# One score chunk in the row-sum banks and one split out-projection step between values and scores

## The chip, the cores and the metric

The kernel runs on one core of one Trainium2 chip. The metric is the device time of one execution in microseconds (us). The core's engines work side by side, each through its own queue in program order: TensorE (PE, matrix products; its weight loads are shown apart as PEld), ScalarE (ACT, here exponentials and Gelu), VectorE (DVE, copies, products, reciprocals), GpSimd (POOL, here masks and the issuing of loads) and SyncE (SP, here the stores and the transposing loads). They wait for each other on semaphores.

## The reference

Attention over eight batches with eight heads, 576 tokens and 64 numbers a head, with 16 "beacon" keys put before the 576 own keys, and a causal mask on the own keys; then a gated feed-forward block over all 4608 tokens. Cut to what matters:

```python
k_all = np.concatenate([beacon_k, k], axis=2)          # 592 keys
v_all = np.concatenate([beacon_v, v], axis=2)
scores = scale * np.matmul(q, k_all.transpose(0, 1, 3, 2))
scores = np.where(causal, -1000000000.0, scores)
a = np.exp(scores - scores.max(-1, keepdims=True))
a /= a.sum(-1, keepdims=True) + 1e-09
attn = np.matmul(a, v_all)                             # (8, 8, 576, 64)
x = attn.transpose(0, 2, 1, 3).reshape(4608, 512)
g, val = x @ w_gate, x @ w_val                         # 512 -> 1536
out = (0.5 * g * (1.0 + erf(g / sqrt(2))) * val) @ w_out   # 1536 -> 512
```

## The kernel before, in words

**Stages.** The kernel takes the batches b = 0 to 7 one after the other. Each has an attention, which leaves 576 columns of `xT_sb` (the transposed input of the feed-forward block), and behind it the twelve gate and value products (`gate_val`) of one chunk of 512 tokens. Nine chunks make 4608 tokens, so that the ninth comes at the very end. The out-projection is cut into units: `o(n)` (line 412) issues the next n units, each one matmul of 128 hidden numbers by 512 outputs; twelve units fill one PSUM bank (tag `o`), and with the twelfth a DVE copy (line 432) and a store are issued. The units of one chunk are strewn into the attention of the next batch, where they fill PE while ACT works. `o(n, cols=64)` (line 421) does a unit as two matmuls, each over half of the array's columns and half of the output's partitions, which run side by side.

**An attention.** Heads are taken in pairs, m = 0 to 3. A pair's scores are made transposed, keys in the partitions, in four chunks (`CHUNKS`, line 31). The order of work is written out by hand as strings that `attention` (line 457) reads step by step, one string a pair and a fifth for the end:

- `Sc`: the scores of chunk c of the pair (`scores`, line 258): matmuls of 64 rows of the array, one for each head of the pair, into a pair of PSUM banks of the pool `s`, which has two such buffers; then one exponential on ACT from there into `expT`; and in batches 2 to 7 the masks of the chunk's diagonal tiles on POOL (`mask`, line 281; the last pair's last chunk is masked on DVE instead). Chunk 0 has the diagonal of key tile 0, chunk 1 those of tiles 2 and 4, chunk 2 that of tile 1, chunk 3 that of tile 3.
- `sc`: the same, with the score banks taken from the tag `z` of another pool, which has one buffer.
- `Zm`: the sums over the keys (`sums`, line 322), with ones as weights, and the values of the first 64 queries. Its two banks are the tag `z`. It takes the key tiles in the order 0, 2, 4, 1, 3 (`attend`, line 305) with matmuls that use 64 columns of the array.
- `Im`: the reciprocals of the sums on DVE (`invert`): a transpose, a reciprocal, a transpose.
- `Vm`: values times weights into the tag `x` (64 columns of the array, too). `Mm`: two DVE products that bring sums and values together (`scale`, line 349); they free `z` and `x`.
- `On`: n units of the out-projection. `Pn`: n units with half the columns each.
- `Nn`: POOL issues n loads of the batch after (`load_next`). In batch 7 nothing is left to load.

Every engine's queue has exactly the order in which these steps are issued. In each of the pairs 1 to 3, then, PE does scores 0 and 1 of pair m, sums and values of pair m-1, scores 2 and 3 of pair m, and then out-projection units. Scores 2 and 3 use the buffers that scores 0 and 1 had, and so wait for the exponentials of those.

For the score banks the rule is in these lines:

```python
s_ps = (psum_s if tag == "s" else psum_x).tile([P, 2, 512], FP32, name="s_ps", tag=tag)
act(expT[:, :, o : o + w], s_ps[:, :, 0:w], ACT.Exp, scale=QK_SCALE)
```

Of the kernel before, what the change touches and what calls it, by code (L numbers as in the profile page):

```python
# [45 lines left out]
Z0 = 448  # L46
# [12 lines left out]
def kernel(  # L59
# [64 lines left out]
    def load_runs(b, m):  # L124
        for out_ap, in_ap in runs(b, m):
            dma(out_ap, in_ap)
# [59 lines left out]
    def load_v_tile(b, t):  # L186
        if t == 0:
            load_beacon(dma, flat(v_ring[b % 2])[0:NB, 0, :], beacon_v[b])
        r0, n = (NB, 112) if t == 0 else (0, KROWS[t])
        dma(v_ring[b % 2][r0 : r0 + n, t, :, :], v[b, :, S_LO[t] : S_LO[t] + n, :].rearrange("h p d -> p h d"))  # L190
# [24 lines left out]
    def heat(n, tag="o"):  # L215
        if n == 0:
            return
        t = bank(tag, FP32, CH, "heat")
        for _ in range(2 * n):
            mm(t[:, 0 : CH // 2], warm[:, 0:P], warm, True, True)  # L220
# [31 lines left out]
    def trans_in(tag, b, m, w):  # L252
        t_ps = bank(tag, BF16, 1024, "t_ps")
        trans(b, m, w, t_ps, [(S, dve_copy)])
# [3 lines left out]
    def scores(b, m, *chunks, tag="s"):  # L258
        i = b * NPAIR + m
        qkT = qk_ring[b % 2]  # L260
        for c in chunks:
            if c == 0:
                exp_of[i] = epool.tile([P, 2, EXP_W], BF16, name="expT", tag="expT")
            expT = exp_of[i]
            s_ps = (psum_s if tag == "s" else psum_x).tile([P, 2, 512], FP32, name="s_ps", tag=tag)
            for t, s_lo, w, col in CHUNKS[c]:
                for hi in range(2):
                    r = slice(64 * hi, 64 * hi + 64)
                    mm(
                        s_ps[:, hi, col : col + w],  # L270
                        qkT[r, 1, m, t * P : (t + 1) * P],
                        qkT[r, 0, m, NB + s_lo : NB + s_lo + w],
                        True,
                        True,
                    )
            o, w = CHUNK_OFF[c], CHUNK_W[c]
            act(expT[:, :, o : o + w], s_ps[:, :, 0:w], ACT.Exp, scale=QK_SCALE)
            if b > 1:
                mask(b, m, c, by_table=m == NPAIR - 1 and c == len(CHUNKS) - 1)
# [42 lines left out]
    def sums(b, m):  # L322
        z_ps = z_of[b * NPAIR + m] = psum_x.tile([P, 1024], FP32, name="z_ps", tag="z")
        attend(b, m, z_ps, Z0, True, 0, SPLIT)
        attend(b, m, z_ps, Z0 + SPLIT, True, SPLIT, S)
        attend(b, m, z_ps, 0, False, 0, SPLIT, start=False)

    def values(b, m):
        x_ps = x_of[b * NPAIR + m] = psum_x.tile([P, S - SPLIT], FP32, name="x_ps", tag="x")
        attend(b, m, x_ps, 0, False, SPLIT, S)  # L330
# [3 lines left out]
    def invert(b, m):  # L334

        i = b * NPAIR + m
        zt = npool.tile([P, S], FP32, name="zt", tag="zt")
        keep(nc.vector.transpose(zt, z_of[i][:, Z0 : Z0 + S]))  # L338
        rz = npool.tile([P, NBLK], FP32, name="rz", tag="rz")
        keep(nc.vector.reciprocal(rz, zt.rearrange("p (n j) -> p n j", j=32)[:, :, 0]))  # L340
        rec = npool.tile([P, S], FP32, name="rec", tag="rec")
        keep(
            nc.vector.transpose(  # L343
                rec.rearrange("p (n j) -> p n j", j=32), rz.unsqueeze(2).to_broadcast([P, NBLK, 32])
            )
        )
        rec_of[i] = rec

    def scale(b, m):
        i = b * NPAIR + m  # L350
        rec = rec_of.pop(i)
        del exp_of[i]
        for acc, q0, q1 in ((z_of.pop(i), 0, SPLIT), (x_of.pop(i), SPLIT, S)):
            keep(
                nc.vector.tensor_tensor(  # L355
                    out=xT_sb[:, m, b * S + q0 : b * S + q1],
                    in0=acc[:, 0 : q1 - q0],
                    in1=rec[:, q0:q1],
                    op=ALU.mult,
                )  # L360
            )
# [50 lines left out]
    def o(n, tags="o", cols=P):  # L412


        for _ in range(n):
            ci, u = divmod(out_done[0], OUT_UNITS)
            ti, fi = divmod(u, F_TILES)
            if fi == 0:
                o_ps_of[0] = bank(tags[out_done[0] // F_TILES % len(tags)], FP32, D_MODEL, "o_ps")
            o_ps = o_ps_of[0][:, 0:D_MODEL]  # L420
            for c0 in range(0, P, cols):
                mm(
                    o_ps[c0 : c0 + cols],
                    h_of[ci][:, fi, ti * P + c0 : ti * P + c0 + cols],
                    wo_sb[:, fi, :],
                    fi == 0,
                    fi == F_TILES - 1,
                    skip_group_check=True,
                )
            if fi == F_TILES - 1:  # L430
                o_sb = opool.tile([P, D_MODEL], FP32, name="o_sb", tag="o_sb")
                keep(nc.vector.tensor_copy(o_sb, o_ps))  # L432
                n0 = ci * CH + ti * P
                keep(nc.sync.dma_start(out=out[n0 : n0 + P, :], in_=o_sb))
            out_done[0] += 1
# [15 lines left out]
    def exp_table():  # L451
        keep(nc.scalar.preload_act_table_set(SET_EXP))

    def gelu_table():
        keep(nc.scalar.preload_act_table_set(SET_GELU))

    def attention(b, *slots, extra=None):


        for m, slot in enumerate(slots):  # L460
            for step in slot.split():
                kind, n = step[0], step[1:]
                if kind == "S":
                    scores(b, m, *(int(c) for c in n))
                elif kind == "s":
                    scores(b, m, *(int(c) for c in n), tag="z")
                elif kind == "Z":
                    sums(b, int(n or m - 1))
                    if not n:
                        invert(b, m - 1)  # L470
                elif kind == "I":
                    invert(b, int(n))
                elif kind == "V":
                    values(b, int(n or m - 1))
                    if not n:
                        scale(b, m - 1)
                elif kind == "M":
                    scale(b, int(n))
                elif kind == "O":
                    o(int(n))  # L480
                elif kind == "P":
                    o(int(n), cols=P // 2)
                elif kind in "adkq":
                    extra[kind](b, *n)
                else:
                    extra[kind](*n) if kind in "kqrwLhyad" else extra[kind](n)
# [40 lines left out]
    def load_next(n):  # L527
        for _ in range(min(n, len(queue))):
            dma(*queue.pop(0))

    W_CUT = ((0, 512), (512, 1024), (1024, 1536))
    extra = {
        "k": lambda b, m, tag: trans_in(tag, b, int(m), 1),
        "q": lambda b, m, tag: trans_in(tag, b, int(m), 0),
        "a": lambda b, m, c: mask(b, int(m), int(c)),
        "d": lambda b, m, c: mask(b, int(m), int(c), by_table=True),
        "r": lambda m: load_runs(0, int(m)),
        "h": lambda n, tag: heat(int(n), tag),
        "y": lambda t: load_v_tile(0, int(t)),
        "N": lambda n: load_next(int(n)),  # L540
# [3 lines left out]
    for m in range(1, NPAIR):  # L544
# [4 lines left out]
        extra=extra,  # L549
# [12 lines left out]
    for b in range(1, B):  # L562
        exp_table()
        if b + 1 < B:
            queue.extend(qk_loads(b + 1))
        if b == 1:
            attention(b, "k1x S0 N3 S1 a01 k3z d00 q1x S2 a02 s3 q2o d03", "S0 S1 k2o Z0 a11 S2 I0 a12 V0 a10 M0 S3", "a13 S0 q3o S1 a21 Z1 S2 a20 I1 S3 a22 V1", "M1 S0 S1 a23 Z2 I2 V2 a31 M2 a30 S2 a32 S3 d33 O12", "Z3 I3 V3 M3 O12 N3 N3", extra=extra)
        elif b == 2:
            attention(b, "O12 s0 S1 S2 O12 S3 N3", "S0 S1 Z0 I0 V0 M0 S2 S3 O12 N3", "S0 S1 Z1 I1 V1 M1 S2 S3 O12 N3", "S0 S1 Z2 I2 V2 M2 S2 S3 O12 N2", "Z3 I3 V3 M3", extra=extra)
        else:  # L570
            attention(b, "O7 s0 S1 S2 O12 S3 N3", "S0 S1 Z0 I0 V0 M0 S2 S3 O12 N3", "S0 S1 Z1 I1 V1 M1 S2 S3 O7 N3", "S0 S1 Z2 I2 V2 M2 S2 S3 P5 N2", "Z3 I3 V3 M3", extra=extra)
        gelu_table()
        if b + 1 < B:
            load_next(99)
            load_v(b + 1)
        gate_val_first(b, o, 0 if b == 1 else 5 if b == 2 else 5)
        if b + 1 < B:
            xbar_transpose(b + 1)
        gate_val(b, 1, F_TILES)
# [36 lines left out]
```

## Time and profile before

| | |
|---|---|
| time, median of 4 runs | 396.21 us (396.01 to 396.74) |
| profiled execution, its own time | 396.2 us |
| its span, first to last instruction | 394.5 us |
| mean granted TensorE clock | 0.995 |
| PE busy | 379.2 us (96%) |
| DVE, ACT, POOL busy | 198.0, 188.1, 161.1 us |
| attention of batch 4, first score to first gate product | 179.28 to 198.32 us |
| attention of batch 7 | 306.65 to 325.68 us |

Rows of the profile give the line of the kernel, the engine, the operation, output and inputs by name, the tile's shape and the count, then busy time and the mean duration. `64*128` before a matmul's shape is rows by columns of the array that it uses. Almost all matmuls are issued by the helper of line 203, so that they are told apart by their outputs: `s_ps` scores, `z_ps` sums, `x_ps` values, `o_ps` out-projection, `gv_ps` gate and value. A row of the timeline gives the start, the length from the first start to the last end, the engine, and in brackets how long the engine had been idle and for what; neighbouring instructions of one kind are merged and bear the shape of the first. A matmul's row ends when its result is there, while the next one starts long before that: what a matmul costs in a row of matmuls is the distance of the starts (0.216 us for an out-projection unit, whose own row has 0.379).

### The profile page before, as it was taken

What the parts mean: (1) busy time and instruction counts of PE and PEld (TensorE: products, weight loads), DVE (VectorE), ACT (ScalarE), POOL (GpSimd) and SP (SyncE); (2) the same over time, 40 slices, a digit from 0 to 9 for tenths busy, and PEclk for the clock granted to TensorE, in tenths of its full rate; (3) what the DMA queues carried; (4) which work ended last, traced back from release to release, by engine and by line L of the source; (5) the groups of instructions that cost most, each with busy time, mean ns of one, the idle gap of its engine ahead of it and who ended that gap; (6) DMA issues with size and microseconds to landing.
All of it is one profiled execution on the core that took longest, in us unless ns stands there. A gap on an engine that the chain in (4) does not pass through costs nothing.

```text
span 394.5 us, 6776 instructions
## 1 busy us (share of the span) xinstructions
PE 379.2 (96%) x2672; PEld 180.2 (46%) x2713; DVE 198.0 (50%) x346; ACT 188.1 (48%) x255; POOL 161.1 (41%) x292
## 2 busy tenths in 40 slices
PE   7899989999999999999999999999999999999996
PEld 4544454444444444444444444444444444444443
DVE  4674587343664448344654367345733475333332
ACT  4653394337633566338733764356533772322210
POOL 8877248503970079204950299008920330000000
PEclk9899999999999999999999999999999999999999
DMA  9999957971999059922995099907991100000012
GB/s 138 165 206 189 179 33 69 166 99 57 107 148 130 0 83 142 155 36 65 112 158 82 28 121 131 135 17 84 138 143 34 56 28 27 0 28 27 28 61 100
DMA packets 139424, 36.50 MB, mean 93 GB/s; under 512 B 126976, under 2 KB 134912, under 8 KB 139392
## 3 DMA queue, kind: packets, MB, share of 16 engines
q0 software_dynamic: 103696, 18.85, 62.8%
q1 hardware_dynamic: 35552, 17.08, 20.2%
q8 instruction: 21, 0.34, 0.4%
q10 hardware_dynamic: 144, 0.13, 0.1%
q14 instruction: 11, 0.09, 0.1%
HBM read 38.27 MB, written 9.44 MB: 121 GB/s over the span
## 4 chain that ended last, share of the span: by engine, by line
PE 89%; DVE 4%; ACT 2%; issue 1%; DMA 1%; POOL 1%; POOLq 0%
PE gv_ps L203 47%; PE o_ps L203 24%; PE z_ps L203 7%; PE s_ps L203 5%; PE x_ps L203 5%; ACT expT L206 2%; DMA k<-in_k_dram 1%; DVE o_sb L432 1%; DVE rec L343 1%; DVE zt L338 1%; PE t_ps L224 1%; DVE xT_sb L355 0%; DVE qkT L247 0%; POOL q L115 0%; DVE rz L340 0%
## 5 line engine op out<-in xcount | busy, mean ns | idle before, releaser
L206 ACT ACTIVATE ge_sb<-gv_ps 128x512 bf16<-128x512 f32 x108 | 64.4, 597 | 152.3 <-PE gv_ps L203 152.3
L390 DVE TENSOR_TENSOR hT_sb<-gv_ps,ge_sb 128x512 bf16<-128x512 f32 x108 | 74.6, 691 | 120.2 <-ACT ge_sb L206 120.2
L206 ACT ACTIVATE expT<-s_ps 128x1024 bf16<-128x1024 f32 (+3 forms) x128 | 102.4, 864 | 31.9 <-PE s_ps L203 30.1
L294 POOL TENSOR_SCALAR_AFFINE_SELECT expT<-expT 128x256 bf16<-128x256 bf16 (+2 forms) x149 | 54.2, 395 | 149.5 <-ACT expT L206 147.5
L203 PE MATMUL gv_ps<-xT_sb,wv_sb 128*128 128x512 bf16 x423 | 111.7, 379 | 0.5
L203 PE MATMUL gv_ps<-xT_sb,wg_sb 128*128 128x512 bf16 x423 | 111.6, 379 | 0.6 <-issue 0.2
L203 PE MATMUL o_ps<-wo_sb,hT_sb 128*128 128x512 bf16 (+2 forms) x446 | 99.7, 374 | 1.5
L203 PEld LDWEIGHTS <-wv_sb 128*128 128x128 bf16 x432 | 42.3, 98 | 50.9
L203 PEld LDWEIGHTS <-wg_sb 128*128 128x128 bf16 x432 | 41.6, 98 | 50.8 <-issue 1.9
L203 PEld LDWEIGHTS <-hT_sb 128*128 128x128 bf16 (+1 forms) x469 | 42.1, 99 | 48.6 <-issue 3.5
L203 PE MATMUL s_ps<-qkT 64*128 64x80 bf16 (+5 forms) x384 | 37.7, 284 | 5.5 <-ACT expT L206 4.5
L432 DVE COPY o_sb<-o_ps 128x512 f32<-128x512 f32 x35 | 24.1, 689 | 36.2 <-PE o_ps L203 34.8
L338 DVE STREAM_TRANSPOSE zt<-z_ps 128x576 f32<-128x576 f32 x32 | 25.0, 781 | 23.7 <-PE z_ps L203 23.7
L115 POOL DMA_DIRECT2D v_sb<-in_v_dram x40 | 33.9, 883 | 0.0
L203 PE MATMUL z_ps<-expT,ones 80*64 80x80 bf16 (+5 forms) x384 | 30.1, 290 | 0.5 <-DVE xT_sb L355 0.3
L115 POOL DMA_DIRECT2D k_sb<-in_k_dram x30 | 25.7, 856 | 7.7 <-DMA wo_sb<-in_moe_w_out_dram 7.4
L203 PEld LDWEIGHTS <-qkT 64*128 64x128 bf16 x384 | 13.9, 94 | 32.2 <-issue 28.4
L203 PE MATMUL x_ps<-expT,v_sb 128*64 128x512 bf16 (+4 forms) x320 | 27.5, 300 | 0.0
L115 POOL DMA_DIRECT2D q_sb<-in_q_dram x30 | 25.9, 863 | 0.3
L343 DVE STREAM_TRANSPOSE rec<-rz 128x576 f32<-128x576 f32 x32 | 24.9, 778 | 1.1
L355 DVE TENSOR_TENSOR xT_sb<-x_ps,rec 128x512 bf16<-128x512 f32 x32 | 21.8, 680 | 0.8 <-PE x_ps L203 0.8
L203 PEld LDWEIGHTS <-ones 128*64 128x64 bf16 (+1 forms) x384 | 15.4, 111 | 12.5 <-issue 6.5
(39 smaller groups left out, 125.5 us busy)
## 6 DMA issues: line engine op xcount, KB each, us to landing
out_dram<-o_sb SPq DMA_DIRECT2D x35, 256.0 KB, 2.0
v_sb<-in_v_dram POOLq DMA_DIRECT2D x24, 128.0 KB, 6.9
q_sb<-in_q_dram POOLq DMA_DIRECT2D x24, 128.0 KB, 4.3
k_sb<-in_k_dram POOLq DMA_DIRECT2D x18, 128.0 KB, 4.4
wg_sb<-in_moe_w_gate_dram POOLq DMA_DIRECT2D x3, 512.0 KB, 7.5
wv_sb<-in_moe_w_val_dram POOLq DMA_DIRECT2D x3, 512.0 KB, 9.7
wo_sb<-in_moe_w_out_dram POOLq DMA_DIRECT2D x1, 1536.0 KB, 13.4
q<-in_q_dram POOLq DMA_DIRECT2D x7, 144.0 KB, 5.3
```

The source lines that it names most:

```text
L115: keep(nc.gpsimd.dma_start(out=out_ap, in_=in_ap))
L203: keep(nc.tensor.matmul(out_ap, lhsT, rhs, start=start, stop=stop, **kw))
L206: keep(nc.scalar.activation(out_ap, in_ap, func, **kw))
L224: keep(nc.tensor.transpose(out_ap, in_ap, ident[0:n, 0:n]))
L294: nc.gpsimd.affine_select(out=d, in_=d, pattern=[[0, 2], [1, DIAG[t]]], compare_op=ALU.is_ge, fill=0.0, base=base, channel_multiplier=-1,)
L338: keep(nc.vector.transpose(zt, z_of[i][:, Z0 : Z0 + S]))
L343: nc.vector.transpose(rec.rearrange("p (n j) -> p n j", j=32), rz.unsqueeze(2).to_broadcast([P, NBLK, 32]))
L355: nc.vector.tensor_tensor(out=xT_sb[:, m, b * S + q0 : b * S + q1], in0=acc[:, 0 : q1 - q0], in1=rec[:, q0:q1], op=ALU.mult,)
L390: nc.vector.tensor_tensor(out=h_of[ci][:, fi, :], in0=gv_ps[:, 1, :], in1=ge_sb, op=ALU.mult)
L432: keep(nc.vector.tensor_copy(o_sb, o_ps))
```

## The change

In the attentions of batches 2 to 7, chunk 3 of pair 0 gets its score banks from the tag `z` (`s3` in place of `S3`). In pairs 1 to 3 one out-projection unit in the half-column form (`P1`) is put between the values of the pair before and scores 2, and the number of units behind scores 3 is changed: one fewer in pairs 1 and 2 of batch 2 and in pair 1 of the others; two fewer in pair 2 of batches 3 to 7; in pair 3, 11 units and these in half-column form for batch 2, and the same five for batches 3 to 7. Each attention issues as many units as before: 60 in batch 2, 43 in the others. The instructions on DVE, ACT, POOL and SP and their order stay as they are.

```diff
         elif b == 2:
-            attention(b, "O12 s0 S1 S2 O12 S3 N3", "S0 S1 Z0 I0 V0 M0 S2 S3 O12 N3", "S0 S1 Z1 I1 V1 M1 S2 S3 O12 N3", "S0 S1 Z2 I2 V2 M2 S2 S3 O12 N2", "Z3 I3 V3 M3", extra=extra)
+            attention(b, "O12 s0 S1 S2 O12 s3 N3", "S0 S1 Z0 I0 V0 M0 P1 S2 S3 O11 N3", "S0 S1 Z1 I1 V1 M1 P1 S2 S3 O11 N3", "S0 S1 Z2 I2 V2 M2 P1 S2 S3 P11 N2", "Z3 I3 V3 M3", extra=extra)
         else:
-            attention(b, "O7 s0 S1 S2 O12 S3 N3", "S0 S1 Z0 I0 V0 M0 S2 S3 O12 N3", "S0 S1 Z1 I1 V1 M1 S2 S3 O7 N3", "S0 S1 Z2 I2 V2 M2 S2 S3 P5 N2", "Z3 I3 V3 M3", extra=extra)
+            attention(b, "O7 s0 S1 S2 O12 s3 N3", "S0 S1 Z0 I0 V0 M0 P1 S2 S3 O11 N3", "S0 S1 Z1 I1 V1 M1 P1 S2 S3 O5 N3", "S0 S1 Z2 I2 V2 M2 P1 S2 S3 P5 N2", "Z3 I3 V3 M3", extra=extra)
```

## The prediction

> **What bounds the kernel now.** The page first: PE is busy for 96% of the span at a clock of 0.995, and the chain that ended last, by engine, is PE:
>
> ```profile
> PE 89%; DVE 4%; ACT 2%; issue 1%; DMA 1%; POOL 1%; POOLq 0%
> ```
>
> No matmul is taken away, so only PE's waits inside the changed attentions can give time. The list of waits has them all:
>
> ```profile
> PE s_ps L203 <- ACT expT L206: 4.5, 13, 0.4
> ```
>
> It counts only idle time after the modelled end of a matmul, so I read the starts instead, in batch 4's timeline (batches 2, 3, 5, 6, 7 repeat it within 0.01 us where I say nothing else). Around pair 0's end, PE, ACT and POOL:
>
> ```profile
> 182.81 0.48 PE L203 MATMUL s_ps<-qkT 64*128 64x208 bf16 x4
> 183.69 0.38 PE L203 MATMUL s_ps<-qkT 64*128 64x64 bf16 x6 [0.39 <-ACT expT L206]
> 184.00 0.22 PE L203 MATMUL z_ps<-expT,ones 128*64 128x64 bf16 x2
> ...
> 183.12 0.52 ACT L206 ACTIVATE expT<-s_ps 128x416 bf16<-128x416 f32 x1 [0.61 <-PE s_ps L203]
> ...
> 183.70 0.41 POOL L294 TENSOR_SCALAR_AFFINE_SELECT expT<-expT 128x256 bf16<-128x256 bf16 x1 [0.73 <-ACT expT L206]
> ```
>
> The first row is S3 of pair 0 and S0 of pair 1 (S0 starts at 182.91). S1 of pair 1 wants the buffer of S3 and starts 0.05 after S3's exponential ends (183.64). In pairs 2 and 3, where it does not wait so, S1 follows S0 by 0.22. So it would start at 183.14: it waits 0.55 us. The sums Z0 follow at 184.00. Tile 3's mask, on POOL, is done at 184.11.
>
> The second wait is in pairs 2 and 3. S2 starts at 190.72, and S3 (208 wide) at 191.07:
>
> ```profile
> 190.72 0.61 PE L203 MATMUL s_ps<-qkT 64*128 64x464 bf16 x4
> 191.07 0.27 PE L203 MATMUL s_ps<-qkT 64*128 64x208 bf16 x2
> 191.27 1.69 PE L203 MATMUL o_ps<-wo_sb,hT_sb 128*128 128x512 bf16 x6
> ...
> 191.13 0.94 ACT L206 ACTIVATE expT<-s_ps 128x928 bf16<-128x928 f32 x1
> ```
>
> S3 starts 0.34 behind S2; in pair 1 it is 0.20. The missing 0.14 is S1's exponential, which ends at 191.02, 0.05 before.
>
> The third place is the end, where Z3 needs the masks of pair 3. POOL's queue, from pair 2's masks on:
>
> ```profile
> 191.09 1.87 POOL L294 TENSOR_SCALAR_AFFINE_SELECT expT<-expT 128x224 bf16<-128x224 bf16 x5
> 193.04 0.90 POOL L115 DMA_DIRECT2D q_sb<-in_q_dram  x1
> 193.92 0.89 POOL L115 DMA_DIRECT2D k_sb<-in_k_dram  x1
> 194.78 0.90 POOL L115 DMA_DIRECT2D q_sb<-in_q_dram  x1
> ...
> 196.64 0.43 POOL L294 TENSOR_SCALAR_AFFINE_SELECT expT<-expT 128x256 bf16<-128x256 bf16 x1
> ```
>
> and PE and DVE beside it:
>
> ```profile
> 196.69 0.98 PE L203 MATMUL z_ps<-expT,ones 128*64 128x64 bf16 x12
> ...
> 197.12 0.55 PE L203 MATMUL z_ps<-expT,ones 128*64 128x464 bf16 x4
> ...
> 196.32 0.22 DVE L355 TENSOR_TENSOR xT_sb<-z_ps,rec 128x64 bf16<-128x64 f32 x1
> ```
>
> POOL has no pause from 191.09 to 197.07. Z3's matmul over tile 1 starts at 197.12, 0.05 behind the end of tile 1's mask. The same distance is there in every batch that loads: 154.61 and 154.67 in batch 3, 239.53 and 239.58 in 5, 281.98 and 282.04 in 6. Only batch 7, without loads, has room (mask end 324.16, matmul 324.48), and batch 2, with longer pairs (mask end 110.45, Z3 at 111.85). So in batches 3 to 6 PE and POOL arrive together, and this decides what PE's earlier gains are worth.
>
> **The change, part by part, in batch 4.**
>
> *s3.* S1 of pair 1 now takes the buffer of S2, whose exponential ended at 182.51, and starts at 183.14. The wait does not vanish: Z0 wants the `z` banks, held by S3 until 183.64. S1's three pairs of matmuls take 0.30 (188.87 to 189.17 in pair 2), so Z0 would be ready at 183.44. What it loses after the release: S1's wait cost 0.05. But Z0 waits with its weight load for the banks, as Z3 does, and that row is nearer: DVE's product ends at 196.54, Z3 starts at 196.69, 0.15 later. I take 0.15: Z0 at 183.78, a gain of 0.22 (0.31 with 0.05). Behind Z0 nothing new waits: its last matmul, 0.65 on, needs tile 3's mask, which ends at 184.11.
>
> *P1.* Behind the values the array is already cut into 64 columns. Values to scores costs 0.096 beyond the 0.087 of the last value matmul (0.183 between starts), and that change of shape is there once before and once after. P1 adds the distance of two such units, 0.213 to 0.216 (row of P5, 195.75 to 195.96), against 0.216 for the unit it replaces; so nothing on its own. Its two weight loads per unit are 0.110 each, the whole-array one 0.098; in P5's row they lie beside the matmuls. P1 opens a new bank in pair 1: the copy that frees it ends at 183.61, P1 comes at 185.24. In pair 2 (batch 2) and the others the bank was freed as early or is already open. No DMA is issued by a unit but the store at a bank's twelfth, which stays at the end of a pair, so SP's queue is passed by nothing, and POOL's loads keep their place behind the masks.
> The Trainium skill, "TensorEngine Tiling (Array Packing)", section Tile-to-Partition Mapping (Restrictions), says that column tiling disables fast weight load, which speaks against putting units into this form. If the loads were not hidden, a unit would cost its two loads, some 0.22, as an estimate from the row, which is what it costs anyway; by the row it costs 0.216, and the sum is the same to 0.01 a unit.
>
> *Pair 1.* S2 starts at 185.56 - 0.22 + 0.21 = 185.55, S3 at 185.75, and S1's exponential is done at 185.41. Then 11 units instead of 12: the pair ends 0.23 earlier.
>
> *Pair 2.* S0, S1, Z1, V1 move by 0.23, S2 by 0.02, but S1's exponential ends at 190.79 and S3 follows at 190.91: 0.16 earlier. With O5 for O7 pair 3 begins 0.59 earlier (with O11 for O12, in batch 2, 0.38). Z1's masks have 0.6 us of room (188.52 for 189.17).
>
> *Pair 3.* S0 at 192.29 needs S2's exponential of pair 2, which moves with S2 to 192.06: fine. S1 at 192.52 needs S3's, 192.47 plus 0.05: just met. Z2's last mask (192.96) is wanted at 193.47. The P1 costs 0.21, S3's wait of 0.14 and Z3's own bank wait of 0.08 (P5 to Z3 0.29, not 0.21) pay it; DVE's chain from Z2 to the product that frees `z` moves with Z2. So PE and DVE could do Z3 0.59 earlier. (The mask of pair 3's last chunk, on DVE, 197.06 to 197.34 now, moves with it.)
>
> *Z3 in batches 3 to 6.* POOL cannot. Pair 2's last two masks wait for S2's and S3's exponentials, which move by 0.02 only, since P1 is ahead of them. Three loads (2.7 us) and four masks (1.4) follow without pause. So tile 1's mask ends at 197.05 and its matmul starts at 197.10. Only the last step shrinks: before, the matmul of tile 3 stood 0.27 behind (197.39), held by DVE's mask; DVE is now early, and the distance is the usual 0.195. It starts at 197.30: 0.09 gained of 0.59. What is late next is POOL.
>
> *Batch 7:* no loads, tile 1's mask follows ACT: ready at 323.84 for a matmul at 323.89. It keeps 0.59.
>
> *Batch 2:* 0.23 (pair 1), 0.15 and 0.15 (pairs 2 and 3), and P11 to Z3 has no change of shape (0.096), less 0.02 for the first distance in P's row: 0.60. POOL is idle before its masks there.
>
> *After the attention* PE runs gate products without a wait; the last product before them is freed by DVE's chain, which moves by at least as much. Sum: 0.60 + 0.59 + 4 x 0.09 = 1.55 us. The profiled execution is 396.2 (its span and 1.7 around it), as the median: 396.2 - 1.55 = **394.65 us**.
>
> Bounds: with 0.05 at Z0 every batch gains 0.09 more, POOL's chain included (6 x 0.09): 394.1. With no gain at Z0, batches 2 and 7 keep 0.38 each; in 3 to 6 P1 then delays pair 2's exponentials by 0.21, and Z3 stands 0.14 later: 0.76 - 0.56, 396.0.
>
> **Rivals.**
> - *POOL does not hold Z3* (its loads finish sooner, or the 0.05 is chance): every attention gains 0.59, 396.2 - 6 x 0.59 = 392.7. Four batches with the same 0.05 speak against it.
> - *The wait only moves to Z0*, as worked out: 396.0, no change to be told.
> - *Slower:* Z0 waits for the whole of pair 0's masks, to 184.16, 0.16 later than now. Then pair 2's exponentials come 0.37 later, and so do POOL's loads and Z3: 4 x 0.30 lost, 2 x 0.22 kept: 397.0. With d the delay of Z0 against 184.00 the sum is 6d - 0.2: it decides from d = 0.03 on. Against it: Z0 now starts at 184.00, before that mask ends (184.11).
>
> **How the numbers follow.** About 0.2% (0.8 us) can be told from no change. Forecast 0.72, its own range 394.1 to 395.4, with a tenth of it inside 0.8 us; POOL free 0.10; wait moved 0.11; slower 0.07. Faster: 0.65 + 0.10, and a little of the moved wait, 0.77. Same 0.15, slower 0.08. Leaving out the slower rival and POOL's, the range is 393.9 to 396.0.
>
> **What the profile would show.** S1 of pair 1 0.22 behind S0; Z0 some 0.15 behind the end of S3's exponential; S3 0.20 behind S2 in pairs 2 and 3; Z3's matmuls in batches 3 to 6 each just behind a POOL mask, at 53 ns; the attention of batch 7 shorter by about 0.6 and of batch 4 by 0.1. I am wrong if POOL's chain starts elsewhere than at S3's mask of pair 2, if P1 brings another change of shape, or if Z0's wait is dearer than its row.

## The result and the profile after

| | before | after |
|---|---|---|
| time, median | 396.28 us (61 runs) | 394.59 us (40 runs) |
| ratio, 95% interval | | 0.9955 (0.9945 to 0.9964) |
| profiled execution: span | 394.5 us | 393.2 us |

The kernel is faster by 0.45%, which is 1.78 us by the ratio (the two medians are 1.69 apart); 1.55 was forecast. Single executions scatter by some 2 us, and the profiles show where: in what comes before batch 2. Batch 0's attention takes 18.94 us in one profile and 18.13 in the other, and starts 1.3 us later, though nothing is changed there. From batch 2 on, lengths repeat within 0.01 us from batch to batch (3 to 6), and what lies between the attentions is the same in both profiles. So below I compare the lengths of attentions 2 to 7 (first score to first gate product, starts of the timeline) of the profiled executions:

| attention of batch | 2 | 3 | 4 | 5 | 6 | 7 | sum |
|---|---|---|---|---|---|---|---|
| before, us | 21.56 | 19.04 | 19.04 | 19.04 | 19.04 | 19.03 | |
| after, us | 20.83 | 18.93 | 18.93 | 18.94 | 18.93 | 18.39 | |
| difference | -0.72 | -0.11 | -0.11 | -0.11 | -0.12 | -0.65 | -1.82 |
| forecast | -0.60 | -0.09 | -0.09 | -0.09 | -0.09 | -0.59 | -1.55 |

The chain that ended last, by engine, from the page after:

```profile
PE 79%; POOL 7%; DVE 4%; ACT 4%; issue 3%; DMA 1%; POOLq 0%
```

POOL had 1% of it before. The list of PE's waits after (us in total, times, longest one), its lines for scores and sums:

```profile
PE s_ps L203 <- ACT expT L206: 2.3, 7, 0.4
...
PE z_ps L203 <- ACT expT L206: 1.1, 6, 0.2
...
PE z_ps L203 <- POOL expT L294: 0.7, 4, 0.2
```

The scores' waits are halved; in their place stand six waits of the sums for ACT, one in each changed attention, and four for POOL's masks, one in each of batches 3 to 6. (The list also has `PE o_ps L203 <- issue: 1.0, 6, 0.2`. That is no wait: in pair 1 of each changed attention the trace has weight loads for 11 units behind scores 3, but matmul records for 10, and the first one's is missing.)

Around pair 0's end in batch 4, PE and ACT (0.35 us earlier than before at the attention's start):

```profile
182.46 0.69 PE L203 MATMUL s_ps<-qkT 64*128 64x208 bf16 x10
183.34 0.22 PE L203 MATMUL z_ps<-expT,ones 128*64 128x64 bf16 x2 [0.19 <-ACT expT L206]
...
182.76 0.52 ACT L206 ACTIVATE expT<-s_ps 128x416 bf16<-128x416 f32 x1 [0.61 <-PE s_ps L203]
```

S3, S0 and S1 are now one row of ten matmuls without a pause. Z0 starts 0.05 behind the exponential (183.28), 0.78 behind S0 (182.56); before it was 1.09. P1 and what follows it, in pair 2:

```profile
189.87 0.25 PE L203 MATMUL x_ps<-expT,v_sb 128*64 128x208 bf16 x2
189.96 0.38 PE L203 MATMUL o_ps<-wo_sb,hT_sb 128*64 128x512 bf16 x2
190.27 0.46 PE L203 MATMUL s_ps<-qkT 64*128 64x464 bf16 x4
190.66 0.39 PE L203 MATMUL o_ps<-wo_sb,hT_sb 128*128 128x512 bf16 x1
```

Values to unit 0.09, unit to S2 0.31, S2 to S3 0.21 (S3 starts at 190.48), all without a wait. And Z3 with POOL and DVE beside it:

```profile
195.69 0.22 PE L203 MATMUL z_ps<-expT,ones 128*64 128x64 bf16 x2
...
196.05 0.50 PE L203 MATMUL z_ps<-expT,ones 128*64 128x336 bf16 x4
196.73 0.39 PE L203 MATMUL z_ps<-expT,ones 128*64 128x464 bf16 x2 [0.18 <-POOL expT L294]
...
195.91 0.36 POOL L294 TENSOR_SCALAR_AFFINE_SELECT expT<-expT 80x160 bf16<-80x160 bf16 x1
196.19 0.49 POOL L294 TENSOR_SCALAR_AFFINE_SELECT expT<-expT 128x256 bf16<-128x256 bf16 x1
...
196.05 0.37 DVE L291 TENSOR_TENSOR expT<-expT,tri 128x256 bf16<-128x256 bf16 x1
```

PE is at Z3 0.65 us sooner than before (195.69 against 196.69, less 0.35), and then stands in front of POOL's masks: the matmul over tile 4 (196.32) starts 0.05 behind the end of its mask (the row 80x160, 196.27), and the one over tile 1 starts 0.05 behind the end of its own (196.68), as before.

### The profile page after: what moved, and what is told of

Same layout as the page of the kernel before. It is cut to its first block, busy times and chain, and to the rows that moved or that the text cites. A ratio compares the mean times of both kernels' runs of the same rounds, so it can differ in the third digit from the quotient of the medians.

```text
span 393.2 us, 6835 instructions
## 1 busy us (share of the span) xinstructions
PE 378.1 (96%) x2702; PEld 181.1 (46%) x2742; DVE 199.3 (51%) x346; ACT 188.1 (48%) x255; POOL 161.3 (41%) x292
## 4 chain that ended last, share of the span: by engine, by line
PE 79%; POOL 7%; DVE 4%; ACT 4%; issue 3%; DMA 1%; POOLq 0%
PE gv_ps L203 47%; PE o_ps L203 19%; PE z_ps L203 5%; PE x_ps L203 4%; ACT expT L206 4%; POOL expT L294 3%; PE s_ps L203 3%; POOL q_sb L115 2%; POOL k_sb L115 2%; DVE o_sb L432 1%; PE t_ps L224 1%; DMA p<-in_q_dram 1%; DVE rec L343 1%; DVE zt L338 1%; DVE qkT L247 1%
## 5 line engine op out<-in xcount | busy, mean ns | idle before, releaser
L203 PE MATMUL gv_ps<-xT_sb,wv_sb 128*128 128x512 bf16 x423 | 111.7, 379 | 0.5
L203 PE MATMUL gv_ps<-xT_sb,wg_sb 128*128 128x512 bf16 x423 | 111.6, 379 | 0.6 <-issue 0.2
L203 PE MATMUL o_ps<-wo_sb,hT_sb 128*128 128x512 bf16 (+2 forms) x476 | 101.5, 374 | 2.1 <-issue 1.0
L203 PEld LDWEIGHTS <-wv_sb 128*128 128x128 bf16 x432 | 42.2, 98 | 51.0
L203 PEld LDWEIGHTS <-hT_sb 128*128 128x128 bf16 (+1 forms) x498 | 42.6, 100 | 48.7 <-issue 5.6
L203 PEld LDWEIGHTS <-wg_sb 128*128 128x128 bf16 x432 | 41.5, 98 | 50.9 <-issue 1.9
L203 PE MATMUL s_ps<-qkT 64*128 64x80 bf16 (+5 forms) x384 | 34.9, 284 | 3.3 <-ACT expT L206 2.3
L203 PE MATMUL z_ps<-expT,ones 80*64 80x80 bf16 (+5 forms) x384 | 31.0, 286 | 2.4 <-ACT expT L206 1.1
L203 PE MATMUL x_ps<-expT,v_sb 128*64 128x512 bf16 (+4 forms) x320 | 27.5, 300 | 0.0
L203 PEld LDWEIGHTS <-qkT 64*128 64x128 bf16 x384 | 13.8, 94 | 26.9 <-issue 22.3
L203 PEld LDWEIGHTS <-ones 128*64 128x64 bf16 (+1 forms) x384 | 15.0, 110 | 15.3 <-issue 6.3
```

The costliest lines, as they stand in the source:

```text
L203: keep(nc.tensor.matmul(out_ap, lhsT, rhs, start=start, stop=stop, **kw))
```

## The experiments

**s3 alone.**

```diff
-"O7 s0 S1 S2 O12 S3 N3"     # the strings before; batch 2 likewise
+"O7 s0 S1 S2 O12 s3 N3"
```

> Only chunk 3 of pair 0 goes to the z banks; no P1, unit counts as before. Theory (PE's gain counts only as far as POOL's masks of pair 3 let it): Z0 0.31 us earlier (0.05 behind S3's exponential, as in the changed kernel). Without P1 pair 2's exponentials come 0.29 earlier too. Batches 2 and 7 gain 0.29 each. In batches 5 and 6 POOL stood idle for 0.3 us in pair 2's masks, so its queue can follow, 0.29 each; in batches 3 and 4 that idle time was under 0.1, so about 0.1 each. Sum 1.3 to 1.4 us: ratio 0.9966. Rival (PE alone decides): 6 x 0.31 = 1.9 us, ratio 0.995. Rival of the wait that only moves: 0, ratio 1.000.

Measured: ratio 0.9928 (0.9904 to 0.9953), which has the scatter of the beginning in it; the attentions are shorter by 0.28 us each, all six, 1.69 in all. So the wait does not only move. Between the theory (1.3 to 1.4, with 0.1 in batches 3 and 4) and "PE alone decides" (0.31 in each, 1.9) this run does not tell: all six gain the same, also those where POOL was to hold Z3, because POOL's queue could follow. In batches 3 to 7 Z3's matmul over tile 3, the last of the sums, starts 0.05 behind DVE's mask (17.83 us from the attention's start, the mask ends at 17.78; 18.11 and 18.06 before). P1 alone and the moved loads, below, tell the two apart. In batches 3 and 4 I had expected 0.1, because POOL seemed to have little idle time there. POOL's queue from pair 2's masks on in this run:

```profile
189.19 1.76 POOL L294 TENSOR_SCALAR_AFFINE_SELECT expT<-expT 128x224 bf16<-128x224 bf16 x5
190.88 0.90 POOL L115 DMA_DIRECT2D q_sb<-in_q_dram  x1
```

From the first mask to the load 1.69 us; before, it was 1.95 (191.09 to 193.04). POOL's records overlap by about 0.08 where it runs straight through. Before, the records of the last two masks of pair 2 only touch the ones in front of them, and both masks start 0.07 behind the end of their exponential (192.08 and 192.49): short waits for ACT, which the merged row does not show. The load behind them starts 0.48 after the last mask's start, here 0.35. "No pause" was read wrongly: there was 0.26 to give.

That one edit has 1.69 of the whole change's 1.82. What P1 adds in batches 2 and 7 (0.44 and 0.37) it takes back in 3 to 6 (4 x 0.17).

**P1 alone.**

```diff
-"O7 s0 S1 S2 O12 s3 N3"     # the strings after; batch 2 likewise
+"O7 s0 S1 S2 O12 S3 N3"
```

> P1 and the changed unit counts, but chunk 3 of pair 0 in the s banks as before. Theory (POOL holds Z3): S1's wait of 0.55 in pair 1 stays; pairs 2 and 3 lose S3's wait, so batches 2 and 7 gain about 0.4 each. In batches 3 to 6 P1 puts pair 2's exponentials 0.21 later, POOL's loads and masks follow, and Z3 comes 0.14 to 0.2 later: a loss of 0.6 to 0.8 in all. Sum: between a gain of 0.2 and nothing, ratio 0.9995 to 1.000. Rival (PE alone decides): S3's wait and the unit moved, 6 x 0.38 = 2.3 us, ratio 0.994.

Measured: ratio 0.9986 (0.9968 to 1.0004). Attention 2 is 0.41 shorter, 7 is 0.34 shorter, 3 to 6 are 0.20 longer each: sum +0.04. This is what "POOL holds Z3" forecast; "PE alone decides" would have shortened all six. POOL in batch 4:

```profile
190.23 1.06 POOL L294 TENSOR_SCALAR_AFFINE_SELECT expT<-expT 128x224 bf16<-128x224 bf16 x3
191.51 0.81 POOL L294 TENSOR_SCALAR_AFFINE_SELECT expT<-expT 128x256 bf16<-128x256 bf16 x2 [0.22 <-ACT expT L206]
192.40 0.90 POOL L115 DMA_DIRECT2D q_sb<-in_q_dram  x1
```

The 0.22 us in brackets is P1: the last two masks of pair 2 wait for exponentials that come one unit later, then the three loads, then pair 3's masks. The same edit shortens attention 7, which has no loads, and attention 2, whose pairs are longer, and lengthens the four in which Z3 waits for POOL.

**The three loads behind pair 3**, in the kernel after and in the kernel before:

```diff
-"... P1 S2 S3 O5 N3", "... P1 S2 S3 P5 N2"
+"... P1 S2 S3 O5", "... P1 S2 S3 P5 N5"       # after, batches 3 to 7
-"... S2 S3 O7 N3", "... S2 S3 P5 N2"
+"... S2 S3 O7", "... S2 S3 P5 N5"             # before, batches 3 to 7
```

> The changed kernel, with the three loads that POOL issues behind pair 2 in batches 3 to 7 issued behind pair 3 instead. Theory (POOL holds Z3): pair 3's masks no longer stand behind 2.7 us of loads; batches 3 to 6 gain 0.6 each instead of 0.11, like batch 7: 2.0 us less than the changed kernel, about 392.5, ratio to before 0.9905; Z3's matmuls start without a mask just ahead of them. Rival (the 0.05 us behind a mask is chance, batches 3 to 6 are held by something else): as the changed kernel, ratio 0.9955.

> The kernel before, with the same three loads issued behind pair 3 instead of pair 2. Theory: there PE, DVE and POOL reach Z3 together, and DVE's chain holds Z3 by itself, so nothing is gained: ratio 0.999 to 1.000. Rival (the loads on POOL cost time by themselves, whatever PE does): about as much gained as by the same move in the changed kernel, ratio 0.995.

Measured, in the kernel after: 392.27 us, ratio 0.9882 (0.9860 to 0.9904). Attentions 3 to 6 are 0.66 shorter than before, like 7 (0.65); the sum is 4.00. POOL, batch 4's end:

```profile
192.04 0.38 POOL L294 TENSOR_SCALAR_AFFINE_SELECT expT<-expT 128x224 bf16<-128x224 bf16 x1 [0.92 <-ACT expT L206]
192.91 0.68 POOL L294 TENSOR_SCALAR_AFFINE_SELECT expT<-expT 128x256 bf16<-128x256 bf16 x2 [0.48 <-ACT expT L206]
194.21 0.41 POOL L294 TENSOR_SCALAR_AFFINE_SELECT expT<-expT 128x256 bf16<-128x256 bf16 x1 [0.62 <-ACT expT L206]
194.69 0.90 POOL L115 DMA_DIRECT2D q_sb<-in_q_dram  x1
```

Now POOL waits for ACT ahead of each chunk's masks, and the masks are early: tile 1's ends at 194.62, its matmul starts at 194.72.

In the kernel before, the same move gives 0.00 in each of attentions 2 to 6 and 0.01 in 7. (The ratio of the whole, 0.9975 with 0.9954 to 0.9996, lies between the theory's 0.999 to 1.000 and the rival's 0.995. In the profiled executions the difference, 0.6, stands wholly before batch 2; that this holds for the medians, too, is not shown.) POOL's mask over tile 1 does end 0.28 sooner in batch 4, but Z3's matmul over tile 3 still starts 0.05 behind DVE's mask, 18.11 from the attention's start in both kernels. So the loads cost nothing until PE and DVE arrive earlier, and then all of it: there were two holds at Z3, less than 0.1 us apart.

**Whole units instead of halves between values and scores**, on top of the loads behind pair 3:

```diff
-"S0 S1 Z0 I0 V0 M0 P1 S2 S3 ..."     # all six places
+"S0 S1 Z0 I0 V0 M0 O1 S2 S3 ..."
```

> The changed kernel with pair 2's loads behind pair 3, and the unit between values and scores 2 over all 128 columns instead of two halves. Theory (a change of the array's shape between matmuls costs PE 0.095 us, and the half form saves one change a unit): values to unit 0.18 between starts instead of 0.09, and 3 x 0.095 = 0.26 to 0.29 us longer for every attention of batches 2 to 7 than with half units (shortened by 0.66 to 0.72 against before); so they are 0.38 to 0.45 shorter than before, 1.6 us in all given back. Rival (the form is of no consequence, only the unit's place counts): attentions as with half units, 0.66 to 0.72 shorter.

> The kernel of the run before with whole units between values and scores 2, once more, for a profile at full clock (that one had 0.756). Theory: values to unit 0.18 between starts instead of 0.09, attentions 0.38 to 0.45 shorter than before. Rival: 0.66 to 0.72 shorter, as with half units.

Measured: ratio 0.9958 (0.9934 to 0.9983). The lengths are from the second one, a single execution at a clock of 0.999: attention 2 is 0.40 shorter than before, 3 to 7 are 0.33 to 0.34 shorter. That gives back 0.32 of each, a little more than the expected 0.26 to 0.29. PE in pair 2:

```profile
189.22 0.63 PE L203 MATMUL x_ps<-expT,v_sb 128*64 128x336 bf16 x8
189.78 0.39 PE L203 MATMUL o_ps<-wo_sb,hT_sb 128*128 128x512 bf16 x1
190.11 0.46 PE L203 MATMUL s_ps<-qkT 64*128 64x464 bf16 x4
```

The last value matmul starts at 189.60: 0.18 to the unit and 0.32 to the scores, where the half form has 0.09 and 0.31. The 0.10 us more stand where the array's shape changes, and come three times an attention; the last 0.02 of the 0.32 are not accounted for. With whole units little is left of what P1 brings beyond s3 alone (attention 7: 0.33 against 0.28).

**No P1 in pair 2.**

```diff
-"... M1 P1 S2 S3 O5 N3"      # batches 3 to 7
+"... M1 S2 S3 O6 N3"
```

> The changed kernel without P1 in pair 2 of batches 3 to 7 (that unit goes behind scores 3 again). Theory (in batches 3 to 6 P1 ahead of pair 2's scores 2 delays pair 2's last masks, with them POOL's loads and Z3): attentions 3 to 6 are 0.28 to 0.33 shorter than before, instead of 0.11, although PE gets back a wait of 0.14 in pair 2; attention 7, where POOL has no loads, loses that 0.14: 0.5 shorter than before instead of 0.65. Rival (POOL's queue does not pass P1's delay on): every attention of 3 to 7 loses 0.14, so 3 to 6 are no shorter than before.

Measured: ratio 0.9937 (0.9915 to 0.9959). Attentions 3 to 6 are 0.26, 0.30, 0.38 and 0.39 shorter than before, not 0.11; attention 7 is 0.52 shorter, not 0.65. Giving PE its wait back makes four attentions faster, and the one without loads slower. The four differ among themselves by POOL's queue: its mask over tile 1 ends 17.60, 17.56, 17.49 and 17.48 us from the attention's start, and PE's matmul over tile 1 starts 0.05 behind in each. In batches 3 and 4 POOL is 0.3 us late from pair 1 on, behind an idle time of 0.33 and 0.41 ahead of a load in pair 0; why it idles there is open. DVE's mask takes longer in these four than its usual 0.28; in batch 4, POOL's mask over tile 1 and DVE's:

```profile
195.88 0.43 POOL L294 TENSOR_SCALAR_AFFINE_SELECT expT<-expT 128x256 bf16<-128x256 bf16 x1
...
196.00 0.46 DVE L291 TENSOR_TENSOR expT<-expT,tri 128x256 bf16<-128x256 bf16 x1
```

**The last mask on POOL.**

```diff
-mask(b, m, c, by_table=m == NPAIR - 1 and c == len(CHUNKS) - 1)
+mask(b, m, c, by_table=False)
```

> The changed kernel with pair 3's last mask on POOL instead of DVE. In the changed kernel POOL's mask over tile 1 of pair 3 takes 0.49 us in batch 4 and DVE's mask beside it 0.37, where they take 0.43 and 0.28 one after the other in the kernel before. Theory (they lengthen each other when they overlap): POOL's tile 1 mask is back at 0.41 to 0.44 and its matmul in Z3 starts 0.06 earlier; the last matmul of the sums then waits for the mask of tile 3 on POOL, so that the attention is about 0.1 longer all the same. Rival (the longer mask has to do with the time at which it runs): 0.49 stays.

POOL and PE, batch 4:

```profile
196.68 0.42 POOL L294 TENSOR_SCALAR_AFFINE_SELECT expT<-expT 128x256 bf16<-128x256 bf16 x1
197.04 0.42 POOL L294 TENSOR_SCALAR_AFFINE_SELECT expT<-expT 128x256 bf16<-128x256 bf16 x1
...
197.16 0.63 PE L203 MATMUL z_ps<-expT,ones 128*64 128x464 bf16 x4
```

Measured on one execution. With no DVE mask beside it the mask over tile 1 is back at 0.42, and its matmul comes 0.35 behind the one before it instead of 0.41. The attention is 0.10 longer all the same (0.01 shorter than before), since tile 3's mask is now in POOL's queue, too.

**One more unit, before the sums.** On top of the loads behind pair 3:

```diff
-"O7 s0 S1 S2 O12 s3 N3", "S0 S1 Z0 I0 V0 M0 P1 ..."      # batch 2 likewise
+"O7 s0 S1 S2 O11 s3 N3", "S0 S1 P1 Z0 I0 V0 M0 P1 ..."
```

> The changed kernel with pair 2's loads behind pair 3, and in addition one unit of pair 0's twelve, in half form, put between scores 1 and the sums Z0 of pair 1. Theory (Z0 waits 0.25 for the exponential of pair 0's chunk 3, which this unit covers, and S3 and its exponential come one unit sooner): attentions 0.2 shorter than with the loads late alone, 0.87 against before in batches 3 to 7; 5.2 us in all, ratio 0.987 or less. Rival (the exponentials bound pair 1, so the next scores wait instead): no more than with the loads late alone, 0.66 an attention.

Measured: 391.16 us, ratio 0.9873 (0.9842 to 0.9904). Attentions 3 to 7 are 0.87 to 0.88 shorter than before, 2 is 0.94; sum 5.30. PE in batch 4:

```profile
179.96 0.69 PE L203 MATMUL s_ps<-qkT 64*128 64x208 bf16 x10
180.57 0.41 PE L203 MATMUL o_ps<-wo_sb,hT_sb 128*64 128x512 bf16 x2
180.83 0.91 PE L203 MATMUL z_ps<-expT,ones 128*64 128x64 bf16 x12
```

The unit stands where Z0 waited, and Z0 follows it by 0.26. By the attentions this is the fastest version that was run, and its time is 1.3% below the kernel before. (The ratio's interval overlaps with that of the loads alone, 0.9860 to 0.9904.)

## Why the prediction was right, point by point

- **The wait at pair 0's end.** It moved from S1 to Z0 and shrank, as said. The term "what it loses after the release" was mis-sized: Z0 starts 0.05 behind the exponential, not 0.15, so that the gain is 0.31 instead of 0.22. The row of Z3, which I took as the nearest, has an extra wait instruction of 0.05 on the weight load's queue (196.58 to 196.63), then the weight load (196.66) and the matmul (196.69); at Z0 there is none, and the cheaper end of the bounds held. With the 0.09 more, batches 2 and 7 would gain 0.69 and 0.68; they gained 0.72 and 0.65, and these last 0.03 each are not accounted for.
- **P1.** No cost of its own: 0.09 from the values and 0.31 to the scores, against 0.18 from values to scores without it, so 0.22 for a unit of 0.216. The rule of the Trainium skill ("TensorEngine Tiling (Array Packing)", Tile-to-Partition Mapping) that column tiling has no fast weight load costs nothing that shows here. The same page's Key Properties say that a change of tiling mode drains the engine; the 0.10 us that the whole form costs where the shape changes agree with that, though no run shows a drain as such.
- **Pairs 2 and 3.** S3 is 0.21 behind S2 in both; the 0.14 is gone.
- **Z3 in batches 3 to 6.** The step that carried the forecast: PE is 0.65 us early, POOL is not. The loads moved in the two kernels show it to be the cause (0.66 instead of 0.11 in one, 0.00 in the other), and P1 alone shows the path (POOL's 0.22 us of waiting in pair 2). The size came out at 0.11 for 0.09 by two errors that offset each other, which is luck. POOL's chain is earlier by about 0.10, not 0.02, as Z0 gained more; but the mask over tile 1 takes 0.49 instead of 0.43, since DVE, now early, runs its own mask at the same time. And "POOL has no pause" was wrong by the 0.26 that s3 alone shows; with P1 in place these masks wait for their exponentials all the same, so the forecast did not suffer.
- **Rivals.** "POOL does not hold Z3" would have given 0.59 in each attention; it needed the loads moved (0.66). "The wait only moves to Z0" and the slower one (Z0 waits for all of pair 0's masks) fall by Z0's start at 183.34, while the last of these masks runs until 183.75. The slower rival's path is real, though: P1 alone, without the gain at Z0, has lengthened batches 3 to 6 by 0.20.
- **Range and sum.** 394.59 lies 0.06 from the forecast, closer than the terms deserve: in the attentions 1.82 came where 1.55 was forecast. With 0.05 at Z0 the prediction's own bound is 0.54 more, 2.09 in all; the longer masks of POOL, 4 x 0.06, are most of what is missing from it.

## What to carry to other kernels

When a wait on the busiest engine is taken away, follow the gain to the next point where several queues meet, and read each queue's slack there: here two were almost equally late, and four of six attentions kept a sixth of what they could have had, until three load issues on a third engine were moved. A filler put ahead of a producer delays all that hangs on that producer; look at who else waits for it, beyond the engine with the gap. And take lengths of repeated stages instead of whole times when the effect is smaller than the scatter of the whole.

## What the runs showed of the hardware that was not expected

- Masks on POOL and DVE lengthen each other when they overlap by enough: POOL's over tile 1 from 0.43 to 0.49 us and DVE's from 0.28 to 0.37, in all four batches of the kernel after where they meet and in neither of the two where they do not. It is the one that starts second whose end moves. In the rows of the kernel after, DVE's mask starts within POOL's mask over tile 4 and ends 0.15 behind its end (196.42 against 196.27); POOL's mask over tile 1 starts within DVE's and ends 0.26 behind its end (196.68). Without P1 in pair 2 POOL's mask over tile 1 comes first and stays at 0.43, and DVE's takes 0.51, 0.46, 0.39 and 0.38 in batches 3 to 6. However long it took, DVE's mask ends 0.15 behind the end of POOL's, in these four and in the four of the kernel after (0.147 to 0.155); where that would come before its own 0.28 are over, as in s3 alone, it stays at 0.28. The Trainium skill, "SBUF — State Buffer", section "SBUF: two separate sides", says that a DVE operation with two inputs in SBUF and a GpSimd operation that reads SBUF take a shared port in turns, each for its whole length. An end at a fixed distance behind the other's end agrees with such turns; the records overlap all the same, and the port itself is seen in no trace.
- Records of neighbouring POOL masks overlap by about 0.08 us when it runs straight through; records that only touch are a sign of a wait (s3 alone: 1.69 us from the first of five masks to the load, where records overlap, against 1.95 before, where some only touch).
